# A decode block with its two small inputs in one layout, loaded by two transfers, and its output stored by two queues

## Chip, core and metric

The kernel runs on one core of a Trainium2 chip. Five engines work side by side: TensorE (PE, its weight loads PEld), VectorE (DVE), ScalarE (ACT), GpSimd (POOL) and SyncE (SP), which here only issues transfers. Sixteen DMA engines move data between the chip's memory (HBM) and the on-chip buffer. The metric is the device time of one execution in microseconds (us); of several runs the median counts.

## What is computed

A transformer block for two sequences with one new token each (B = 2, D = 512): a modulated attention over a window of the key and value caches, then a modulated feed-forward layer. All data are float32.

```python
mod = (silu(c) @ w_mod).reshape(2, 6, 1, 512)
sa, ca, ga, sb, cb, gb = (mod[:, i] for i in range(6))
h = layernorm(x) * (1 + ca) + sa
q = heads(h @ wq)                      # 32 heads of 128, 8 key/value heads
k, v = k_cache[:, :, -4096:], v_cache[:, :, -4096:]
x = x + ga * (softmax(q k^T / sqrt(128)) v @ wo)
h = layernorm(x) * (1 + cb) + sb
x = x + gb * (silu(h @ w1) @ w2)       # w1: 512 x 1792, w2: 1792 x 512
```

The inputs that matter for the time are w_mod (6 MB), wq and wo (8 MB each), the two cache windows (32 MB each) and w1 and w2 (3.5 MB each). x and c are 2 x 512 numbers, 4 KB each, and so is the output.

## The kernel before

Every large load goes through a ring of eight buffers of 2 MB (`RING`, `stream`), and all are issued in order by SP: w_mod in four parts, wq in four, then for each of the eight key/value heads the keys and values of both sequences, then wo in four parts, w1 in three and w2 in five. A load is issued once the buffer eight places back in the ring has been used up.

A vector of 512 numbers is spread over the 128 partitions so that VectorE can turn it with its 32 x 32 transposes. There are two such layouts here. In both, one row out of sixteen partitions holds data (`rows8` picks these eight rows), four rows for each sequence. In the "channel" layout (`c_ch`, `x_ch`, lines 99 to 110) a row a holds, for each k from 0 to 3, the 32 channels that start at 128 k + 32 a; after a transpose, block k holds the channels of rows 128 k to 128 k + 127 of a weight matrix. So `load_rows` (line 72) loads the weight's rows in blocks of 128: partition p of block k holds row 128 k + p. In the "spread" layout (`x_sp`) row g holds the 128 consecutive channels from 128 g on; `turned` (line 268) transposes it reading every fourth column, so that block k holds the channels 4 p + k. The weights that go with it are loaded by `load_runs` (line 91): partition p holds consecutive rows of the matrix. wo, w1 and w2 are loaded like that; w_mod and wq are loaded by `load_rows`.

The head: SP issues the first quarter of w_mod (line 74), then c and x in the channel layout, one transfer for each sequence (line 107, four transfers with pieces of 32 numbers), then the rest of w_mod and wq. DVE transposes c (line 235), silu follows (ACT and DVE), and PE multiplies with w_mod: `m_ch` (line 246) gets shift and scale of the first normalization in the channel layout, which takes a strided view `ab` of the weights, and `m_sp` (line 249) the other four vectors in the spread layout. Meanwhile `moments` computes mean and variance of x. Lines 257 to 263 make the normalized, modulated h_a and its transpose hq_T, from which PE makes q (line 285).

The middle: for each head, DVE transposes the keys (line 337), PE makes the scores (349), ACT the exponentials, and PE the weighted values (423). The order of these instructions is written out by hand (`keep_in_program_order`).

The end: the attention output goes through wo (550, 561). x is loaded a second time, now in the spread layout (line 474, issued between wo and w1), and turned into xT for the second normalization. PE multiplies with w1 (595) and w2 (631, 643); DVE multiplies the result with the gate and adds x (`yo`, lines 653 and 654). SP stores yo with one transfer (line 656).

Of the kernel before, what the change touches and what calls it, by code (L numbers as in the profile page):

```python
# [10 lines left out]
ALU = mybir.AluOpType  # L11
AX = mybir.AxisListType

P = 128
B, D = 2, 512
HQ, HKV, DH = 32, 8, 128
# [7 lines left out]
def adaln_block(  # L24
# [16 lines left out]

    nc = tc.nc
    SK = k_cache.shape[2]
    W = min(4096, max(256, SK // 4))
# [14 lines left out]
    def const(shape, name):  # L63
        return consts.tile(shape, F32, name=name)

    def bank(tag, name):
        return (psum1 if tag in "CO" else psum).tile([P, 512], F32, tag=tag, name=name)

    def stream(name):
        return ring.tile([P, 4096], F32, tag="st", name=name)  # L70

    def load_rows(name, w, k, width):
        t = stream(f"{name}{k}")[:, :width]
        nc.sync.dma_start(t, w[k * P : (k + 1) * P, :])
        return t

    def load_k(b, h):
        t = stream(f"k{h}_{b}")
        nc.sync.dma_start(
            t, k_cache[b, h, SK - W :, :].rearrange("(p n) d -> p (n d)", p=P)  # L80
        )
        return t
# [8 lines left out]
    def load_runs(name, w, per, lo, hi):  # L91

        e = w.shape[1]
        t = stream(f"{name}{lo}")[:, : (hi - lo) * e].rearrange("p (q e) -> p q e", e=e)
        nc.sync.dma_start(t, w.rearrange("(p q) e -> p q e", q=per)[:, lo:hi, :])
        return t


    x2 = x.rearrange("b s d -> (b s) d")
    x_sp, x_ch, c_ch = const([P, P], "x_sp"), const([P, P], "x_ch"), const([P, P], "c_ch")  # L100
    for t in (c_ch, x_ch, x_sp):
        nc.vector.memset(t, 0.0)
    wm = [load_rows("wm", w_mod, 0, 6 * D)]
    rows8 = lambda t: t.rearrange("(ab r) m -> ab r m", r=16)[:, 0, :]
    for t, src in ((c_ch, c), (x_ch, x2)):
        for b in range(B):
            nc.sync.dma_start(
                rows8(t)[b : 2 * 4 : 2, :].rearrange("a (k c) -> a k c", k=4),
                src[b, :].rearrange("(k a c) -> a k c", k=4, a=4),
            )  # L110
    wm += [load_rows("wm", w_mod, k, 6 * D) for k in range(1, 4)]
    wqt = [load_rows("wq", wq, k, HQ * DH) for k in range(4)]


    ident = const([P, P], "ident")
# [47 lines left out]
    for m in range(4):  # L163
        nc.gpsimd.affine_select(
            out=quad,
# [27 lines left out]

    oTn = const([P, 32, 32], "oTn")
    nc.gpsimd.memset(oTn, 0.0)
    mod_ch = const([P, 2, P], "mod_ch")
    mod_sp = const([P, 4, P], "mod_sp")
    x1 = const([P, P], "x1")

    def silu_exp(t, name, shape):  # L200

        e = once.tile(shape, F32, tag="silu", name=name)
        nc.vector.tensor_scalar(e, t, -1.0, 87.0, op0=ALU.mult, op1=ALU.min)
        nc.scalar.activation(e, e, AF.Exp)
        nc.vector.tensor_scalar(e, e, 1.0, None, op0=ALU.add)
        nc.vector.reciprocal(e, e)
        return e

    def moments(t, name):

        st = work.tile([P, 6], F32, tag="st6", name=f"st_{name}")
        nc.vector.bn_stats(st, t)
        mv = work.tile([P, 2], F32, tag="mv", name=f"mv_{name}")
        nc.vector.bn_aggr(mv, st)  # L214
        avgm = avg.rearrange("p a r -> p (a r)")
        sm = bank("B", f"mean_{name}")
        nc.tensor.matmul(sm[:, 0:1], avgm, mv[:, 0:1], start=True, stop=True)  # L217
        mean = work.tile([P, 1], F32, tag="mean", name=f"m_{name}")
        nc.vector.tensor_copy(mean, sm[:, 0:1])
        dm = work.tile([P, 2], F32, tag="dm", name=f"dm_{name}")  # L220
# [12 lines left out]

    cT = const([P, 4, 32], "cT")
    nc.vector.transpose(cT.rearrange("p k r -> p (k r)"), c_ch)
    sg = silu_exp(cT, "sgc", [P, 4, 32])
    scT = const([P, 4, 32], "scT")
    nc.vector.tensor_mul(scT, cT, sg)
    m_ch = bank("A", "m_ch")[:, : 2 * P]
    m_sp = bank("D", "m_sp")  # L240
    for k in range(4):
        ab = wm[k][:, : 2 * D].rearrange("p (s k a c) -> p a s k c", s=2, k=4, a=4)
        cd = wm[k][:, 2 * D :].rearrange("p (s g m) -> p g s m", s=4, g=4)
        for g in range(4):
            r = slice(32 * g, 32 * g + 32)
            nc.tensor.matmul(m_ch[r, :], scT[:, k, :], ab[:, g], start=(k == 0), stop=(k == 3))
        for g in range(4):
            r = slice(32 * g, 32 * g + 32)
            nc.tensor.matmul(m_sp[r, :], scT[:, k, :], cd[:, g], start=(k == 0), stop=(k == 3))  # L249
        if k == 0:  # L250
            mean_a, rstd_a = moments(x_ch, "a")
            xn = once.tile([P, P], F32, tag="xp", name="xn_a")
            nc.vector.tensor_scalar(
                xn, x_ch, mean_a, rstd_a, op0=ALU.subtract, op1=ALU.mult
            )

    nc.vector.tensor_copy(mod_ch[:, 0, :], m_ch[:, :P])
    nc.vector.tensor_scalar(mod_ch[:, 1, :], m_ch[:, P:], 1.0, None, op0=ALU.add)
    h_a = once.tile([P, P], F32, tag="pr", name="h_a")
    nc.vector.tensor_mul(h_a, xn, mod_ch[:, 1, :])  # L260
    nc.vector.tensor_add(h_a, h_a, mod_ch[:, 0, :])
    hq_T = const([P, 4, 32], "hq_T")
    nc.vector.transpose(hq_T.rearrange("p k r -> p (k r)"), h_a)
    nc.scalar.copy(mod_sp.rearrange("p s m -> p (s m)"), m_sp)
    nc.gpsimd.tensor_scalar(mod_sp[:, 2, :], mod_sp[:, 2, :], 1.0, None, op0=ALU.add)
    ga, sb, cb1, gb = (mod_sp[:, s, :] for s in range(4))

    def turned(t, name):
        o = const([P, 4, 32], name)
        nc.vector.transpose(o, t.rearrange("p (m k) -> p k m", k=4))  # L270
        return o


    hT, uT = const([P, 4, 32], "hT_b"), const([P, F // P, 32], "uT")
# [6 lines left out]
    for k in range(4):  # L281
        wv = wqt[k].rearrange("p (n s g m) -> p n g s m", n=2, s=4, g=G)
        for n in range(2):
            for g in range(G):
# [4 lines left out]
                    start=(k == 0),  # L289
                    stop=(k == 3),  # L290
                )
    for n in range(2):
        qT = once.tile([P, D], F32, tag="wide", name=f"qT{n}").rearrange("p (s j r) -> p s j r", s=4, r=32)
        nc.vector.transpose(qT.rearrange("p s j r -> p (s j r)"), q_ps[n])  # L294
        for g in range(G):
            r = slice(32 * g, 32 * g + 32)
# [8 lines left out]
        for i in range(4):  # L305
            r = slice(32 * i, 32 * i + 32)
# [160 lines left out]
    collect(HKV - 1)  # L467

    gaT, sbT, cbT = turned(ga, "gaT"), turned(sb, "sbT"), turned(cb1, "cbT")
    nc.vector.tensor_copy(hT[:, :, 1:32:16], sbT[:, :, 0:32:16])  # L470
    ax = once.tile([P, P], F32, tag="ax", name="ax")
    for q0 in range(0, 32, 8):
        wot.append(load_runs("wo", wo, 32, q0, q0 + 8))
    nc.sync.dma_start(rows8(x_sp), x2.rearrange("b (g m) -> g b m", m=P))
    xT = turned(x_sp, "xT")
    w1t = []
    for lo, hi in ((0, 2), (2, 3), (3, 4)):
# [17 lines left out]
    for r in (0, 64):  # L495
# [4 lines left out]
            start=True,  # L500
            stop=True,
# [46 lines left out]
    for q in range(24):  # L548
        g = q % 4
# [4 lines left out]
            start=(q < 4),  # L554
            stop=(q >= 20),
# [3 lines left out]
    for q in range(24, 32):  # L559
        for g in range(4):  # L560
# [4 lines left out]
                start=(q == 24),  # L565
                stop=(q == 31),
# [26 lines left out]
    for k in range(4):  # L593
        for g in range(4):
# [4 lines left out]
                start=(k == 0),  # L599
                stop=(k == 3),  # L600
# [16 lines left out]
    for b in range(B):  # L617
# [5 lines left out]
            op0=ALU.mult,  # L623
            op1=ALU.add,
# [4 lines left out]
    for tt in range(WIDE):  # L629
        g = tt % 4  # L630
# [4 lines left out]
            start=(tt < 4),  # L635
            stop=(tt >= WIDE - 4),
# [4 lines left out]
    for tt in range(WIDE, T2):  # L641
        for g in range(4):
# [4 lines left out]
                start=(tt == WIDE),  # L647
                stop=(tt == T2 - 1),
# [3 lines left out]
    yo = once.tile([P, P], F32, tag="yo", name="yo")  # L652
    nc.vector.tensor_mul(yo, y, gb)
    nc.vector.tensor_add(yo, yo, x1)
    of = out.rearrange("b s d -> (b s) d")
    nc.sync.dma_start(of.rearrange("b (g m) -> g b m", m=P), rows8(yo))


_INS = ["A_x", "A_k_cache", "A_v_cache", "A_wq", "A_wo", "B_w1", "B_w2", "c", "w_mod"]
# [24 lines left out]
```

## Time and profile before

| What | Value |
|---|---|
| Median of 3 runs | 237.28 us (236.99 to 237.31) |
| The profiled execution's own time | 236.89 us |
| Its span in the profile | 235.0 us |
| Read from HBM | 97.53 MB, 415 GB/s over the span |
| Mean granted clock of TensorE | 0.869 |
| DMA queue of SP | 7592 packets, 97.54 MB |

The span runs from the first to the last event of the profile; the time of a run has some 1.9 us more. "DMA share" in the views is the mean busy share of the sixteen DMA engines in a stretch; since packets overlap it can pass 1. A line such as "A <- B: 1.0" says that A sat idle for 1.0 us until B released it. SPq marks instructions in SP's queue, where the length of a DMA line is the time that issuing takes, not that of the transfer.

### The profile page before, as it was taken

Reading aid. Unit: us, or ns where it says so; the run is one execution under the profiler, and the core shown is the slowest. Engines: PE = TensorE matmul, PEld = TensorE weight load, DVE = VectorE, ACT = ScalarE, POOL = GpSimd, SP = SyncE. Lnnn points to the kernel's source line nnn. Section 1 sums busy time; section 2 is a strip of 40 time slices with the busy share of each in tenths; the row PEclk is TensorE's granted clock in tenths of the full one; section 3 lists DMA queues with packets and bytes.
Section 4 is the critical chain, followed back from the end, with each engine's and each line's share of the span. In section 5 each row is a group of like instructions: output and inputs, shape, how many; then the busy total and the mean of one; then the engine's idle time right before and its main releaser. Section 6 shows DMA issues by size and latency. Waiting matters only on the chain.

```text
span 235.0 us, 2644 instructions
## 1 busy us (share of the span) xinstructions
PE 146.5 (62%) x1094; PEld 45.9 (20%) x1094; DVE 114.6 (49%) x176; ACT 25.4 (11%) x56; POOL 10.3 (4%) x30
## 2 busy tenths in 40 slices
PE   0086546367187577667549519626743967788993
PEld 0032101101011121121112102111211222335332
DVE  0634000793694792693892792595298050002130
ACT  2200000100300200200200200200020021003210
POOL 8600000100000000000000000000000000000000
PEclk9999975759869997999976967965985799999999
DMA  6999999999999999999999999999999999999991
GB/s 253 426 438 427 427 438 427 424 439 427 429 441 424 427 438 427 429 438 424 429 435 429 427 432 432 432 429 432 428 429 429 429 432 429 432 426 422 421 412 56
DMA packets 7603, 97.69 MB, mean 416 GB/s; under 512 B 920, under 2 KB 936, under 8 KB 1576
## 3 DMA queue, kind: packets, MB, share of 16 engines
q1 hardware_dynamic: 7592, 97.54, 97.5%
q8 instruction: 8, 0.13, 0.2%
q14 instruction: 3, 0.02, 0.0%
HBM read 97.53 MB, written 0.00 MB: 415 GB/s over the span
## 4 chain that ended last, share of the span: by engine, by line
DMA 64%; DVE 22%; PE 10%; ACT 2%; issue 1%; SPq 1%; DVEq 0%
DVE kT L337 16%; DMA wo<-in_A_wo_dram 14%; DMA k<-in_A_k_cache_dram 14%; DMA v<-in_A_v_cache_dram 13%; DMA wq<-in_A_wq_dram 13%; DMA w<-in_B_w_dram 7%; PE s L349 5%; DMA wm<-in_w_mod_dram 3%; DVE zp L395 2%; PE o L423 2%; PE q L285 1%; DVE xp L393 1%; ACT pr L381 1%; DVE mx L359 1%; ACT L381 1%
## 5 line engine op out<-in xcount | busy, mean ns | idle before, releaser
L337 DVE STREAM_TRANSPOSE kT<-k 128x1024 f32<-128x1024 f32 x64 | 73.7, 1210 | 1.6 <-DMA k<-in_A_k_cache_dram 1.6
L349 PE MATMUL s<-kT,qbd 128*32 128x512 f32 x256 | 44.5, 670 | 11.2 <-DVE kT L337 11.1
L423 PE MATMUL o<-v,ptb 128*32 128x512 f32 x256 | 38.5, 730 | 19.8 <-DMA v<-in_A_v_cache_dram 19.3
L359 DVE TENSOR_REDUCE mx<-s 128x1 f32<-128x512 f32 x8 | 5.5, 691 | 40.1 <-PE s L349 40.1
L349 PEld LDWEIGHTS s<-kT,qbd 128*32 128x32 f32 x256 | 11.1, 126 | 45.8 <-issue 24.1
L285 PE MATMUL q<-wq,hq_T 128*32 128x512 f32 x64 | 11.2, 836 | 10.1 <-DMA wq<-in_A_wq_dram 10.1
L423 PEld LDWEIGHTS o<-v,ptb 128*32 128x32 f32 x256 | 8.1, 124 | 35.8 <-issue 33.1
L402 PE MATMUL pT<-zp,id 128*32 128x256 f32 x64 | 5.6, 418 | 13.9 <-DVE zp L395 13.9
L379 ACT COPY bias<-bp 128x1 f32<-128x1 f32 x8 | 1.3, 159 | 111.9 <-PE bp L377 111.9
L537 PE MATMUL junk<-selh,id 128*32 128x256 f32 x46 | 11.3, 380 | 0.0
L294 DVE STREAM_TRANSPOSE qT<-q 128x512 f32<-128x512 f32 x2 | 1.4, 718 | 18.6 <-PE q L285 18.3
L395 DVE TENSOR_TENSOR zp<-xp,group 128x1024 f32<-128x1024 f32 x8 | 9.8, 1225 | 0.2
L393 DVE STREAM_TRANSPOSE xp<-pr 128x512 f32<-128x512 f32 x8 | 5.6, 701 | 4.4 <-ACT pr L381 4.4
L217 PE MATMUL mean_a<-mv_a,avg 128*128 128x1 f32 x2 | 0.6, 362 | 10.6 <-DVE mv_a L214 10.6
L361 PE MATMUL mT<-ident,mx 128*1 128x128 f32 x16 | 3.0, 270 | 6.4 <-DVE mx L359 6.4
L550 PE MATMUL acc_o<-wo,oTn 128*32 128x512 f32 x48 | 5.8, 598 | 1.9 <-DMA wo<-in_A_wo_dram 1.6
L537 PEld LDWEIGHTS junk<-selh,id 128*32 128x32 f32 x46 | 5.0, 110 | 6.7 <-issue 3.5
L438 PE MATMUL o_all<-ob,selh 128*64 128x128 f32 x64 | 5.7, 304 | 0.8 <-ACT ob L432 0.8
L270 DVE STREAM_TRANSPOSE xT<-x_sp 128x128 f32<-128x128 f32 x1 | 0.4, 403 | 11.8 <-DMA x_sp<-in_A_x_dram 11.8
L432 ACT COPY ob<-o 128x512 f32<-128x512 f32 x8 | 4.7, 585 | 10.3 <-PE o L423 10.3
L285 PEld LDWEIGHTS q<-wq,hq_T 128*32 128x32 f32 x64 | 2.1, 128 | 18.8 <-DMA wq<-in_A_wq_dram 12.5
L249 PE MATMUL m_sp<-wm,scT 128*32 128x512 f32 x32 | 5.7, 796 | 0.0
(132 smaller groups left out, 95.0 us busy)
## 6 DMA issues: line engine op xcount, KB each, us to landing
k<-in_A_k_cache_dram SPq DMA_DIRECT2D x16, 2048.0 KB, 30.2
v<-in_A_v_cache_dram SPq DMA_DIRECT2D x16, 2048.0 KB, 31.5
wq<-in_A_wq_dram SPq DMA_DIRECT2D x4, 2048.0 KB
wo<-in_A_wo_dram SPq DMA_DIRECT2D x4, 2048.0 KB, 32.3
wm<-in_w_mod_dram SPq DMA_DIRECT2D x4, 1536.0 KB, 10.2
w<-in_B_w_dram SPq DMA_DIRECT2D x2, 1024.0 KB, 23.2
w<-in_B_w_dram SPq DMA_DIRECT2D x1, 1792.0 KB
w<-in_B_w_dram SPq DMA_DIRECT2D x2, 896.0 KB
```

The source lines that it names most:

```text
L249: nc.tensor.matmul(m_sp[r, :], scT[:, k, :], cd[:, g], start=(k == 0), stop=(k == 3))
L285: nc.tensor.matmul(q_ps[n][32 * g : 32 * g + 32, :], hq_T[:, k, :], wv[:, n, g], start=(k == 0), stop=(k == 3),)
L337: inorder(nc.vector.transpose(kT[h, b][:, :, 8 * n4 : 8 * n4 + 8, :].rearrange("p j n k -> p n j k"), kt[h, b][:, n4 * 1024 : (n4 + 1) * 1 ...
L349: inorder(nc.tensor.matmul(s_ps[h][r : r + 32, :], qbd[h // 4][:, h % 4, b, j, :], kT[h, b][:, j, 16 * c : 16 * c + 16, :], start=(j == 0) ...
L359: inorder(nc.vector.tensor_reduce(mx, s_ps[h], axis=AX.X, op=ALU.max))
L393: inorder(nc.vector.transpose(xp, pr[h]))
L395: inorder(nc.vector.tensor_mul(zp, xp[:, None, :, 0:16].to_broadcast([P, 4, 16, 16]), group[:, :, None, None].to_broadcast([P, 4, 16, 16]),))
L402: inorder(nc.tensor.matmul(tp[32 * i : 32 * i + 32, :], id4, zp.rearrange("p a s x -> p (a s) x")[:, :, 4 * i : 4 * i + 4], start=True, st ...
L423: inorder(nc.tensor.matmul(o_ps[h][32 * c : 32 * c + 32, :], ptb[h % 2][:, 256 * b + 32 * w : 256 * b + 32 * w + 32], vt[h, b][:, 512 * w ...
L438: inorder(nc.tensor.matmul(o_all[r : r + 64, :], selh[:, m, HQ - G - G * h : 3 * HQ - G - G * h], o_sb[h][:, m * DH : (m + 1) * DH], start ...
L537: inorder(nc.tensor.matmul(junk[0:32, :256], id4, selh.rearrange("p m y -> p (m y)")[:, :256], start=True, stop=True,))
L550: inorder(nc.tensor.matmul(acc[32 * g : 32 * g + 32, :], oTn[:, q, :], wot[q // 8][:, q % 8, :], start=(q < 4), stop=(q >= 20),))
```

## The change

The channel layout is given up. c and x are each loaded once, in the spread layout (`c_sp`, `x_sp`), by one transfer for both sequences, with pieces of 128 numbers. The second load of x, between wo and w1, is gone. w_mod and wq are loaded by `load_runs` in single rows: partition p of part k holds row 4 p + k, where it held row 128 k + p. `turned` serves c and h_a too, and the first normalization's shift and scale come out in the spread layout (`m_a`, `mod_a`). The number and shape of the matrix products stay. The output is stored by two transfers, the rows of the first sequence from SP's queue and those of the second from ACT's.

```diff
-    x_sp, x_ch, c_ch = const([P, P], "x_sp"), const([P, P], "x_ch"), const([P, P], "c_ch")
-    for t in (c_ch, x_ch, x_sp):
+    x_sp, c_sp = const([P, P], "x_sp"), const([P, P], "c_sp")
+    for t in (c_sp, x_sp):
         nc.vector.memset(t, 0.0)
-    wm = [load_rows("wm", w_mod, 0, 6 * D)]
+    row4 = lambda name, w, k: load_runs(name, w, 4, k, k + 1)[:, 0, :]
+    wm = [row4("wm", w_mod, 0)]
     rows8 = lambda t: t.rearrange("(ab r) m -> ab r m", r=16)[:, 0, :]
-    for t, src in ((c_ch, c), (x_ch, x2)):
-        for b in range(B):
-            nc.sync.dma_start(
-                rows8(t)[b : 2 * 4 : 2, :].rearrange("a (k c) -> a k c", k=4),
-                src[b, :].rearrange("(k a c) -> a k c", k=4, a=4),
-            )
-    wm += [load_rows("wm", w_mod, k, 6 * D) for k in range(1, 4)]
-    wqt = [load_rows("wq", wq, k, HQ * DH) for k in range(4)]
+    for t, src in ((c_sp, c), (x_sp, x2)):
+        nc.sync.dma_start(rows8(t), src.rearrange("b (g m) -> g b m", m=P))
+    wm += [row4("wm", w_mod, k) for k in range(1, 4)]
+    wqt = [row4("wq", wq, k) for k in range(4)]
...
-    cT = const([P, 4, 32], "cT")
-    nc.vector.transpose(cT.rearrange("p k r -> p (k r)"), c_ch)
+    cT = turned(c_sp, "cT")
...
-        ab = wm[k][:, : 2 * D].rearrange("p (s k a c) -> p a s k c", s=2, k=4, a=4)
+        ab = wm[k][:, : 2 * D].rearrange("p (s g m) -> p g s m", s=2, g=4)
...
-            mean_a, rstd_a = moments(x_ch, "a")
+            mean_a, rstd_a = moments(x_sp, "a")
...
-    nc.vector.transpose(hq_T.rearrange("p k r -> p (k r)"), h_a)
+    hq_T = turned(h_a, "hq_T")
...
-    nc.sync.dma_start(rows8(x_sp), x2.rearrange("b (g m) -> g b m", m=P))
     xT = turned(x_sp, "xT")
...
-    of = out.rearrange("b s d -> (b s) d")
-    nc.sync.dma_start(of.rearrange("b (g m) -> g b m", m=P), rows8(yo))
+    for b, queue in enumerate((nc.sync, nc.scalar)):
+        queue.dma_start(out[b, 0, :].rearrange("(g m) -> g m", m=P), rows8(yo)[b : 2 * 4 : 2, :])
```

More of the change, by code (lines that the diff above doesn't have):

```diff
@@ L70, in stream @@
         return ring.tile([P, 4096], F32, tag="st", name=name)
[L72 to L75, printed above, removed]
     def load_k(b, h):
@@ L195, in adaln_block @@
     nc.gpsimd.memset(oTn, 0.0)
-    mod_ch = const([P, 2, P], "mod_ch")
+    mod_a = const([P, 2, P], "mod_a")
     mod_sp = const([P, 4, P], "mod_sp")
@@ L231, in moments, with turned @@
         return mean, rstd
-    cT = const([P, 4, 32], "cT")
-    nc.vector.transpose(cT.rearrange("p k r -> p (k r)"), c_ch)
+    def turned(t, name):
+        o = const([P, 4, 32], name)
+        nc.vector.transpose(o, t.rearrange("p (m k) -> p k m", k=4))
+        return o
+    cT = turned(c_sp, "cT")
     sg = silu_exp(cT, "sgc", [P, 4, 32])
@@ L238, in adaln_block @@
     nc.vector.tensor_mul(scT, cT, sg)
-    m_ch = bank("A", "m_ch")[:, : 2 * P]
+    m_a = bank("A", "m_a")[:, : 2 * P]
     m_sp = bank("D", "m_sp")
     for k in range(4):
-        ab = wm[k][:, : 2 * D].rearrange("p (s k a c) -> p a s k c", s=2, k=4, a=4)
+        ab = wm[k][:, : 2 * D].rearrange("p (s g m) -> p g s m", s=2, g=4)
         cd = wm[k][:, 2 * D :].rearrange("p (s g m) -> p g s m", s=4, g=4)
@@ L245, in adaln_block @@
             r = slice(32 * g, 32 * g + 32)
-            nc.tensor.matmul(m_ch[r, :], scT[:, k, :], ab[:, g], start=(k == 0), stop=(k == 3))
+            nc.tensor.matmul(m_a[r, :], scT[:, k, :], ab[:, g], start=(k == 0), stop=(k == 3))
         for g in range(4):
@@ L250, in adaln_block @@
         if k == 0:
-            mean_a, rstd_a = moments(x_ch, "a")
+            mean_a, rstd_a = moments(x_sp, "a")
             xn = once.tile([P, P], F32, tag="xp", name="xn_a")
             nc.vector.tensor_scalar(
-                xn, x_ch, mean_a, rstd_a, op0=ALU.subtract, op1=ALU.mult
+                xn, x_sp, mean_a, rstd_a, op0=ALU.subtract, op1=ALU.mult
             )
-    nc.vector.tensor_copy(mod_ch[:, 0, :], m_ch[:, :P])
-    nc.vector.tensor_scalar(mod_ch[:, 1, :], m_ch[:, P:], 1.0, None, op0=ALU.add)
+    nc.vector.tensor_copy(mod_a[:, 0, :], m_a[:, :P])
+    nc.vector.tensor_scalar(mod_a[:, 1, :], m_a[:, P:], 1.0, None, op0=ALU.add)
     h_a = once.tile([P, P], F32, tag="pr", name="h_a")
[L260 to L263, printed above, removed]
+    nc.vector.tensor_mul(h_a, xn, mod_a[:, 1, :])
+    nc.vector.tensor_add(h_a, h_a, mod_a[:, 0, :])
+    hq_T = turned(h_a, "hq_T")
     nc.scalar.copy(mod_sp.rearrange("p s m -> p (s m)"), m_sp)
```

4 lines of the change are left out of this document (removed).

## The prediction

> **What bounds the kernel now.** The page comes first: its busy shares, the slices of the DMA rows, and the chain of waits.
>
> ```profile
> span 235.0 us, 2644 instructions
> PE 146.5 (62%) x1094; PEld 45.9 (20%) x1094; DVE 114.6 (49%) x176; ACT 25.4 (11%) x56; POOL 10.3 (4%) x30
> DMA  6999999999999999999999999999999999999991
> DMA packets 7603, 97.69 MB, mean 416 GB/s; under 512 B 920, under 2 KB 936, under 8 KB 1576
> DMA 64%; DVE 22%; PE 10%; ACT 2%; issue 1%; SPq 1%; DVEq 0%
> ```
>
> The reader sees that no compute engine is busy for more than 62% of the span, while the DMA row is full from the second slice to the last but one. The chain still gives DVE 22% and PE 10%: whenever a load waits for a buffer, the chain runs through the engine that frees it. That would matter only if the transfers ever ran dry, so the next view is the DMA share and rate stretch by stretch (columns: stretch, its length, five engines, granted clock, DMA share, GB/s).
>
> ```profile
> 1.60:2.00 0.40, 0.00 (x0) 0.00 (x0) 0.00 (x0) 0.40 (x1) 0.40 (x2) 1.00 1.94 338
> 3.00:6.50 3.50, 0.00 (x0) 0.00 (x0) 0.00 (x0) 0.00 (x0) 3.50 (x10) 1.00 1.04 431
> 6.50:8.00 1.50, 0.00 (x0) 0.00 (x0) 0.91 (x5) 0.00 (x0) 1.50 (x3) 1.00 0.96 401
> 8.00:18.00 10.00, 5.88 (x36) 2.58 (x40) 4.81 (x18) 1.85 (x3) 1.44 (x3) 1.00 1.01 430
> 18.00:37.00 19.00, 10.88 (x84) 2.32 (x76) 2.45 (x9) 0.58 (x1) 0.53 (x1) 0.86 1.01 430
> 40.00:180.00 140.00, 84.97 (x570) 23.39 (x564) 95.76 (x109) 14.99 (x39) 0.94 (x4) 0.83 1.01 431
> 195.00:213.00 18.00, 14.51 (x112) 5.50 (x104) 0.88 (x3) 2.12 (x3) 0.00 (x0) 1.00 1.01 433
> 213.00:229.00 16.00, 14.05 (x151) 6.38 (x150) 4.15 (x19) 2.49 (x5) 0.00 (x0) 1.00 0.99 416
> 229.00:230.00 1.00, 0.98 (x26) 0.67 (x28) 0.00 (x0) 0.21 (x1) 0.00 (x0) 1.00 0.67 270
> 230.00:231.20 1.20, 1.11 (x37) 0.59 (x30) 0.00 (x0) 0.00 (x0) 0.00 (x0) 1.00 0.24 90
> 231.20:233.50 2.30, 0.39 (x8) 0.12 (x8) 0.58 (x2) 0.00 (x0) 0.00 (x0) 1.00 0.00 0
> 233.50:234.00 0.50, 0.00 (x0) 0.00 (x0) 0.00 (x0) 0.00 (x0) 0.00 (x0) 1.00 0.04 8
> 234.00:235.00 1.00, 0.00 (x0) 0.00 (x0) 0.00 (x0) 0.00 (x0) 0.00 (x0) 1.00 0.00 0
> ```
>
> From 3 us to 229 us the sixteen DMA engines are at a share of 0.96 to 1.04 and move 401 to 433 GB/s, whichever load is on the wire. So the time is a sum of three pieces: a start of some 2 to 3 us, the bytes at about 430 GB/s, and a tail after the last load. An edit counts only if it changes the bytes, their rate, the start or the tail.
>
> **The change, part by part.** The first part is the head of SP's queue. Columns here are start, length, engine, line and operation.
>
> ```profile
> 0.73 0.40 SPq L74 DMA_DIRECT2D wm<-in_w_mod_dram  x1
> 1.19 1.29 SPq L107 DMA_DIRECT2D c_ch<-in_c_dram  x2
> 2.53 1.09 SPq L107 DMA_DIRECT2D x_ch<-in_A_x_dram  x2
> 3.65 1.40 SPq L74 DMA_DIRECT2D wm<-in_w_mod_dram  x3
> 181.60 0.58 SPq L474 DMA_DIRECT2D x_sp<-in_A_x_dram  x1
> ```
>
> Four small issues (1.29 + 1.09 = 2.38 us) become two in the form of the row at L474 (2 x 0.58 = 1.16 us), so the second w_mod load is issued about 1.2 us sooner, near 2.4 us. The first load is issued at the same 0.73 us, and it alone keeps the engines at 431 GB/s until 6.5 us; the second is in the queue by then either way. Gain of the earlier issue: nothing, covered by the first w_mod load; without that cover it would be the 1.2 us. The transfers themselves are another matter: the stretch of 6.5 to 8 us, in which the small pieces pass, runs at 401 instead of 430 GB/s, a loss of 1.5 x (1 - 401/430) = 0.10 us. Two loads in place of four should keep half of it: -0.05 us, bounds 0 and -0.10.
>
> The second part is the way in which w_mod and wq are read. A partition still reads one piece of 12 or 16 KB, but neighbours in the tile are now 48 or 64 KB apart in memory instead of adjacent. These loads are 4 x 1536 KB + 4 x 2048 KB = 14.7 MB, 34 us at 431 GB/s. The nearest row is the wo load, which reads 16 KB pieces 64 KB apart (eight rows of 2 KB out of 32 for each partition): its stretch, 195 to 213 us, shows 433 GB/s against 431 for the adjacent k and v pieces of 40 to 180 us and 430 for wq now. Value taken: 0. Bounds: at 433 GB/s the 14.7 MB would gain 0.16 us; at the slowest loading stretch of the trace, 416 GB/s (213 to 229 us, the narrower pieces of w1 and w2), they would lose 1.2 us.
>
> The Trainium skill has a rule against this edit ("DMA: Bandwidth & Descriptors", section "Latency and other measured facts"): a pitch between rows that is a large power of two slows copies, 207 GB/s at 512 KiB where a padded pitch gave 214. Applied at its full 3.4% to 34 us that would be an estimate of +1.15 us; the rows of wo at a 64 KB pitch do not agree, and no run here has a pitch as large as that page's.
>
> The third part is the work between the small loads and q. Transposes that read with a stride cost a little more:
>
> ```profile
> 7.09 0.31 DVE L235 STREAM_TRANSPOSE cT<-c_ch 128x128 f32<-128x128 f32 x1 [5.75 <-DMA c_ch<-in_c_dram]
> 21.37 0.31 DVE L263 STREAM_TRANSPOSE hq_T<-h_a 128x128 f32<-128x128 f32 x1
> 213.28 0.40 DVE L270 STREAM_TRANSPOSE xT<-x_sp 128x128 f32<-128x128 f32 x1 [11.79 <-DMA x_sp<-in_A_x_dram]
> 16.14 5.23 SPq L79 DMA_DIRECT2D k<-in_A_k_cache_dram  x4
> L285 PE MATMUL q<-wq,hq_T 128*32 128x512 f32 x64 | 11.2, 836 | 10.1 <-DMA wq<-in_A_wq_dram 10.1
> ```
>
> cT and hq_T take the form of xT: 0.40 instead of 0.31 us, +0.09 each. In the order of the changed kernel xT itself (0.40 us) moves up between the constants and the first statistics, and the bias of silu stands ahead of the constants. So the DVE head shifts by +0.6 us at most, and by less where silu's exponential now overlaps the constants. Two things wait behind it. PE's q products wait 10.1 us for wq, longer than any such shift. SP's first k loads (16.14 us) wait for the modulation products to free w_mod's buffers; the DMA engines then still hold wq, which keeps them at 430 GB/s to 37 us, a cover of 20 us. Cost: 0; without wq in flight it would be up to 0.6 us. The matmuls into m_a read adjacent columns instead of strided ones, in equal number and shape, under the same cover.
>
> The fourth part is the x load taken out between wo and w1 (0.58 us of SP's queue). It and xT end nothing: SP has the w loads waiting on buffers, and these land late after their issue for want of bandwidth, not of issue.
>
> ```profile
> w<-in_B_w_dram SPq DMA_DIRECT2D x1, 768.0 KB, 20.1
> w<-in_B_w_dram SPq DMA_DIRECT2D x1, 512.0 KB, 16.5
> DVE aoT L572 <- PE ao L561: 2.5, 1, 2.5
> ```
>
> With 16.5 to 20 us from issue to landing, a w load that is issued half a microsecond sooner only queues longer. DVE's next wait after xT was for PE's output product, which stays. Cost and gain 0.
>
> The fifth part is the tail, the one place where nothing covers.
>
> ```profile
> 230.53 1.06 PE L643 MATMUL acc_y<-w,uT 128*32 128x128 f32 x24
> 231.66 0.29 DVE L653 TENSOR_TENSOR yo<-acc_y,mod_sp 128x128 f32<-128x128 f32 x1 [5.73 <-PE acc_y L643]
> 231.98 0.29 DVE L654 TENSOR_TENSOR yo<-yo,x 128x128 f32<-128x128 f32 x1
> 232.30 0.59 SPq L656 DMA_DIRECT2D out_dram<-yo  x1
> SPq L680 <- DMA out_dram<-yo: 1.0, 1, 1.0
> 228.62 0.58 ACT L522 COPY acc_y_sb<-acc_yw 128x512 f32<-128x512 f32 x1 [3.51 <-PE acc_yw L631]
> 181.22 0.33 SPq L95 DMA_DIRECT2D wo<-in_A_wo_dram  x1
> ```
>
> From the end of yo (232.27 us) the store costs 0.59 us of issue, then 1.0 us in which SP waits for its landing; some 1.1 us more pass to the end of the span. After the change each queue issues half the store with one dimension fewer. SP's half lies between 0.33 us (the plain two-dimensional issue of wo) and 0.59 us: a gain of 0 to 0.26 us. ACT's half is an operation the trace does not show; ACT itself is free, its last copy ending at 229.20 us. From below, it costs what SP's does. From above, it comes 0.59 us behind SP's, if the two issues are served one after the other. The end waits for the later one, so the tail moves by -0.26 to +0.59 us. The four kinds of small issues in the trace all took 0.52 to 0.65 us on average, so I hold each half near 0.55 us, side by side: -0.05 us.
>
> The sum, against the profiled execution's 236.89 us (span 235.0 and 1.9 around it): 236.89 - 0.05 (head) + 0 (pitch) - 0.05 (tail) = 236.8 us. That execution ran 0.39 us below the median of the runs shown, so against the median the same sum is 237.28 - 0.1 = 237.2 us.
>
> **The rivals.** *The small loads hold up the engines that end last (faster).* The tail is ragged: between 229 and 231.2 us the engines do 0.67 x 1.0 + 0.24 x 1.2 = 0.96 us of work in 2.2 us, so the last of them ends 1.2 us after an even finish. If the 0.10 us lost on sixteen engines is really 1.6 us on four of them, that is 0.4 us each, and if those are the last, three fifths of five loads saved gives 0.25 us; with SP's 0.26 us in the tail that is 237.28 - 0.5 = 236.8 us. For it: 920 packets under 512 B. Against it: nothing here says which engines end last, and both halves are needed to get past 0.2%.
>
> *ACT's half of the store lands last (slower).* Place: the end of the kernel, after yo. Price: up to 0.59 us, one issue, if the halves are served in turn or if ACT's first transfer takes that much longer than SP's last. It decides as soon as ACT's half lands later than SP's gains. 237.28 - 0.05 + 0.59 = 237.8 us. For it: no transfer leaves ACT's queue anywhere in the trace. Against: ACT is idle, and the halves touch different rows.
>
> *The spread rows cost bandwidth (slower).* 1.2 us by the 416 GB/s stretch: 238.4 us. Against it stands the wo stretch, of the very same pattern as wq's.
>
> *The change does nothing that can be told.* This is the forecast's own class, and the reason for it is the DMA row.
>
> **How the numbers follow.** No change to be told (within 0.2%, or 0.47 us, which is about what a measurement of this kernel can tell from none): 0.51, at 237.2 us. The fast engines' rival: 0.22, at 236.8 us and below. ACT's store: 0.19, at 237.8 us. The spread rows and anything else on the DMA engines: 0.08, near 238.4 us. So faster 0.22, same 0.51, slower 0.27. The range adds the gains' bounds (0.10 + 0.16 + 0.26 = 0.52) below, with a little more for the rival, and reaches above past the store's bound and part of the way to the spread rows: 236.6 to 238.2 us. The forecast's own range is 236.9 to 237.6 us.
>
> **What would show each step.** Head: the three further w_mod issues near 2.4 us, the stretch of 6.5 to 8 us above 401 GB/s, and k still issued near 16 us. Pitch: 430 GB/s in the stretches 8 to 18 and 18 to 37 us; 420 or less would prove the third rival. Tail: yo ending within 0.2 us of 232.27; if it ends 0.3 us sooner at equal rates, the first rival holds. Store: one issue on SP and one on ACT after yo, with 2.6 to 2.75 us from the end of yo to the end of the span; 3.2 us or more there is the ACT rival. The forecast as a whole is wrong if the time leaves 236.8 to 237.75 us, above all if the DMA row shows a slice under 9 before the last.

## The result, and the profile after

The changed kernel takes 237.90 us (median of 7 runs, 237.80 to 238.02) against 237.21 us for the kernel before on the same chip (7 runs, 236.99 to 237.31). The ratio is 1.0031, with a 95% interval of 1.0022 to 1.0040: some 0.7 us slower. That is inside the outer range of 236.6 to 238.2 us, but it is not the forecast of no change, and it lies outside 236.8 to 237.75 us, beyond which the prediction called itself wrong. The profiled execution took 237.90 us with a span of 235.8 us. The profiled execution of before (236.89 us) ran 0.3 us under its median, so that differences between these two profiles come out a little too large. One of the 27 runs of the kernel before that stand beside e5 to e8 below took 289 us and is in no ratio.

The page of the changed kernel first: the DMA rows, the queues, and the chain of waits.

```profile
span 235.8 us, 2641 instructions
DMA  7999999999999999999999999999999999999991
DMA packets 7539, 97.69 MB, mean 414 GB/s; under 512 B 848, under 2 KB 872, under 8 KB 1512
q10 hardware_dynamic: 8, 0.00, 0.0%
DMA 64%; DVE 23%; PE 8%; ACT 2%; issue 1%; POOL 0%; SPq 0%; POOLq 0%
```

The picture is the same: a DMA row that is full from end to end. Fewer small packets pass (848 under 512 B instead of 920), and q10 is new: ACT's queue. So the loss is in the rate, the start or the tail. The stretches of before, now for the changed kernel (stretch, length, five engines, granted clock, DMA share, GB/s):

```profile
3.00:6.50 3.50, 0.00 (x0) 0.00 (x0) 0.00 (x0) 0.00 (x0) 3.50 (x10) 1.00 0.98 402
6.50:8.00 1.50, 0.00 (x0) 0.00 (x0) 0.91 (x4) 0.00 (x0) 1.50 (x3) 1.00 0.99 377
8.00:18.00 10.00, 6.28 (x44) 2.79 (x48) 4.79 (x21) 1.85 (x3) 1.44 (x3) 1.00 1.01 424
18.00:37.00 19.00, 10.04 (x76) 2.25 (x68) 2.45 (x9) 0.58 (x1) 0.53 (x1) 0.84 1.01 433
40.00:180.00 140.00, 84.38 (x564) 23.40 (x556) 95.31 (x108) 14.98 (x39) 0.94 (x4) 0.82 1.01 431
213.00:229.00 16.00, 14.02 (x151) 6.28 (x150) 3.73 (x18) 2.66 (x4) 0.00 (x0) 1.00 1.00 421
```

Until 18 us, while w_mod is on the wire, the rate is 402, 377 and 424 GB/s where it was 431, 401 and 430 (the first two of these vary much from execution to execution, as the experiments show). From 18 us on, where wq, the caches and the last weights pass, nothing is lost. The head of SP's queue and the tail (start, length, engine, line, operation; the last line is a wait):

```profile
2.53 1.43 SPq L88 DMA_DIRECT2D wm<-in_w_mod_dram  x3
4.01 4.02 SPq L88 DMA_DIRECT2D wq<-in_A_wq_dram  x4
15.74 5.04 SPq L72 DMA_DIRECT2D k<-in_A_k_cache_dram  x4
...
232.53 0.29 DVE L641 TENSOR_TENSOR yo<-yo,x 128x128 f32<-128x128 f32 x1
232.85 0.58 SPq L644 DMA_DIRECT2D out_dram<-yo  x1
232.86 1.42 ACTq L644 DMA_DIRECT2D out_dram<-yo  x1
SPq L668 <- DMA out_dram<-yo: 1.2, 1, 1.2
```

The w_mod loads are issued at 2.53 instead of 3.65 us, and k at 15.74 instead of 16.14 us: no issue is late. Yet yo ends at 232.82 instead of 232.27 us, 0.55 us later, and from there to the end of the span it is 3.0 instead of 2.7 us. The issue on ACT takes 1.42 us against 0.58 us on SP. So there are two places to look at: w_mod's loads and the store.

### The profile page after: what moved, and what is told of

It reads as the page before. It is cut to its first block, busy times and chain, and to the rows that moved or that the text cites. A ratio compares the mean times of both kernels' runs of the same rounds, so it can differ in the third digit from the quotient of the medians.

```text
span 235.8 us, 2641 instructions
## 1 busy us (share of the span) xinstructions
PE 147.0 (62%) x1094; PEld 46.0 (20%) x1094; DVE 114.1 (48%) x175; ACT 25.4 (11%) x56; POOL 10.3 (4%) x30
## 4 chain that ended last, share of the span: by engine, by line
DMA 64%; DVE 23%; PE 8%; ACT 2%; issue 1%; POOL 0%; SPq 0%; POOLq 0%
DMA k<-in_A_k_cache_dram 26%; DVE kT L325 16%; DMA wo<-in_A_wo_dram 14%; DMA wq<-in_A_wq_dram 13%; DMA w<-in_B_w_dram 8%; PE s L337 5%; DMA wm<-in_w_mod_dram 3%; DVE zp L383 3%; DVE xp L381 1%; ACT pr L369 1%; DVE mx L347 1%; PE acc_o L537 1%; DVE qT L282 1%; ACT L369 1%; PE mT L349 1%
## 5 line engine op out<-in xcount | busy, mean ns | idle before, releaser
L411 PE MATMUL o<-v,ptb 128*32 128x512 f32 x256 | 40.5, 765 | 21.9 <-DMA v<-in_A_v_cache_dram 21.4
L337 PE MATMUL s<-kT,qbd 128*32 128x512 f32 x256 | 42.2, 659 | 9.5 <-DVE kT L325 9.5
L273 PE MATMUL q<-wq,hq_T 128*32 128x512 f32 x64 | 10.6, 789 | 10.3 <-DMA wq<-in_A_wq_dram 10.3
L537 PE MATMUL acc_o<-wo,oTn 128*32 128x512 f32 x48 | 7.3, 753 | 1.1 <-DMA wo<-in_A_wo_dram 0.7
L365 PE MATMUL bp<-negscale,mrow 1*128 1x1 f32 x16 | 3.0, 256 | 4.2 <-DVE mrow L358 4.2
```

The costliest lines, as they stand in the source:

```text
L273: nc.tensor.matmul(q_ps[n][32 * g : 32 * g + 32, :], hq_T[:, k, :], wv[:, n, g], start=(k == 0), stop=(k == 3),)
L337: inorder(nc.tensor.matmul(s_ps[h][r : r + 32, :], qbd[h // 4][:, h % 4, b, j, :], kT[h, b][:, j, 16 * c : 16 * c + 16, :], start=(j == 0) ...
L411: inorder(nc.tensor.matmul(o_ps[h][32 * c : 32 * c + 32, :], ptb[h % 2][:, 256 * b + 32 * w : 256 * b + 32 * w + 32], vt[h, b][:, 512 * w ...
L537: inorder(nc.tensor.matmul(acc[32 * g : 32 * g + 32, :], oTn[:, q, :], wot[q // 8][:, q % 8, :], start=(q < 4), stop=(q >= 20),))
```

## The experiments

Each kernel was timed against the kernel before on the same chip, 11 runs of it (5 for e7, one for e11) against some 27 to 33. The interval is about 0.2 us to either side (0.3 for e7). The ratio comes from all these runs and is not quite the quotient of the two medians; a price in us below is the ratio's excess times 237 us. e3 to e6, e9 to e11, e14 and e15 leave out the pairing of weight rows and channels, so their output is another; apart from the edit, their loads and products are those of the kernel that they start from, in number and size. The diffs are shortened; in every kernel c and x are issued right behind the first load.

| Run | Edit | Median us (before) | Ratio | 95% interval |
|---|---|---|---|---|
| e1 | changed kernel, one store | 237.56 (237.07) | 1.0017 | 1.0009 to 1.0026 |
| e2 | before, stores on SP and ACT | 237.38 (237.07) | 1.0012 | 1.0004 to 1.0021 |
| e3 | changed kernel, adjacent rows | 237.51 (237.07) | 1.0018 | 1.0009 to 1.0027 |
| e4 | before, w_mod spread | 237.42 (237.07) | 1.0011 | 1.0002 to 1.0020 |
| e5 | before, wq spread | 237.24 (237.24) | 1.0003 | 0.9994 to 1.0012 |
| e6 | before, two small loads | 236.98 (237.24) | 0.9992 | 0.9983 to 1.0001 |
| e7 | before, two stores on SP | 237.82 (237.24) | 1.0032 | 1.0019 to 1.0044 |
| e8 | before, one store on ACT | 237.24 (237.24) | 1.0003 | 0.9995 to 1.0012 |
| e9 | changed kernel, adjacent rows, one store | 237.24 (237.18) | 1.0003 | 0.9994 to 1.0012 |
| e10 | before, wq's rows in w_mod's place | 237.06 (237.18) | 0.9996 | 0.9987 to 1.0004 |
| e11 | before, wq ahead, w_mod spread | 237.19 (237.18) | one run | none |
| e12 | mixed kernel | 237.19 (237.18) | 1.0001 | 0.9992 to 1.0010 |
| e13 | changed kernel, wq ahead, one store | 236.95 (237.21) | 0.9989 | 0.9981 to 0.9998 |
| e14 | before, one part of wq ahead, w_mod spread | 237.04 (237.21) | 0.9993 | 0.9984 to 1.0002 |
| e15 | before, w_mod parts 1 to 3 spread | 237.47 (237.21) | 1.0011 | 1.0002 to 1.0020 |

### The store (e1, e2, e7, e8)

e1 takes the second store out of the changed kernel, e2 puts it into the kernel before, e7 issues both halves from SP, e8 issues the whole store from ACT.

```diff
 e1: changed kernel
-    for b, queue in enumerate((nc.sync, nc.scalar)):
-        queue.dma_start(out[b, 0, :].rearrange("(g m) -> g m", m=P), rows8(yo)[b : 2 * 4 : 2, :])
+    of = out.rearrange("b s d -> (b s) d")
+    nc.sync.dma_start(of.rearrange("b (g m) -> g b m", m=P), rows8(yo))
 e2, e7: kernel before
-    of = out.rearrange("b s d -> (b s) d")
-    nc.sync.dma_start(of.rearrange("b (g m) -> g b m", m=P), rows8(yo))
+    for b, queue in enumerate((nc.sync, nc.scalar)):      # e7: (nc.sync, nc.sync)
+        queue.dma_start(out[b, 0, :].rearrange("(g m) -> g m", m=P), rows8(yo)[b : 2 * 4 : 2, :])
 e8: kernel before
-    nc.sync.dma_start(of.rearrange("b (g m) -> g b m", m=P), rows8(yo))
+    nc.scalar.dma_start(of.rearrange("b (g m) -> g b m", m=P), rows8(yo))
```

> The changed kernel with the output stored by one transfer from SP, as before the change. Theory H (head and tail both pay: the two first w_mod loads of the changed kernel land 0.4 to 0.6 us late, and ACT's store, whose issue takes 1.42 us against SP's 0.58, ends the kernel 0.2 us later): 0.2 us less than the changed kernel, about 237.7 us, +0.5 us on the kernel before (ratio 1.002), and 2.75 us from the end of yo to the end of the span. Rival T (the tail pays for all of it): the time of the kernel before, 237.2 us. Rival N (the second store costs nothing, since SP waits for both anyhow): 237.9 us.

> The kernel before with the output stored by two transfers, from SP and ACT; nothing else is changed. Theory H: +0.2 us (237.4 us, ratio 1.001), an issue on ACT of about 1.4 us, 2.95 us from the end of yo to the end of the span, and the head as before. Rival T: +0.7 us (237.9 us). Rival N: 237.2 us.

> The kernel before with the output stored by two transfers, both from SP, one after the other. Theory A (ACT is the slow one: its issue takes 1.41 us): the second issue costs one SP issue, 0.58 us, less what the halves save, so +0.4 to +0.6 us (ratio 1.002). Rival (any second store costs the same 0.3 us through the second wait at the end): +0.3 us, ratio 1.0012.

> The kernel before with the one store issued by ACT instead of SP. Theory A: ACT's issue takes 1.4 us against 0.59 and the end comes 0.3 to 0.8 us later, ratio 1.0012 to 1.0035. Rival (the cost is in having two stores, not in ACT): 237.1 us, ratio 1.000.

e1 keeps a loss of 0.4 us (1.0017), so the tail is not all of it. e2 has 1.0012, or 0.28 us: the second store has its price without any other edit. e7 pays more, 0.76 us (1.0032, five runs; 0.45 to 1.04), of which one more issue on SP is some 0.57 us (1.15 us for two). e8 was to be 0.3 to 0.8 us slower if ACT were the slow one, and is not (1.0003). The tails of the three kernels, e2 first: when the issues ran, and two stretches with the bytes of the store in them.

```profile
232.31 0.58 SPq L657 DMA_DIRECT2D out_dram<-yo  x1
232.31 1.41 ACTq L657 DMA_DIRECT2D out_dram<-yo  x1
...
233.40:233.80 0.40, 0.00 (x0) 0.00 (x0) 0.00 (x0) 0.00 (x0) 0.00 (x0) 1.00 0.02 5
233.80:234.20 0.40, 0.00 (x0) 0.00 (x0) 0.00 (x0) 0.00 (x0) 0.00 (x0) 1.00 0.03 5
```

e7, both halves from SP:

```profile
232.29 1.15 SPq L657 DMA_DIRECT2D out_dram<-yo  x2
...
233.50:234.00 0.50, 0.00 (x0) 0.00 (x0) 0.00 (x0) 0.00 (x0) 0.00 (x0) 0.50 0.02 4
234.00:234.50 0.50, 0.00 (x0) 0.00 (x0) 0.00 (x0) 0.00 (x0) 0.00 (x0) 0.50 0.02 4
```

e8, the whole store from ACT:

```profile
232.27 1.14 ACTq L656 DMA_DIRECT2D out_dram<-yo  x1
...
233.40:233.80 0.40, 0.00 (x0) 0.00 (x0) 0.00 (x0) 0.00 (x0) 0.00 (x0) 1.00 0.04 10
233.80:234.20 0.40, 0.00 (x0) 0.00 (x0) 0.00 (x0) 0.00 (x0) 0.00 (x0) 1.00 0.00 0
```

ACT's issue is long, 1.14 us, but alone it puts all 4 KB on the wire before 233.80 us. With SP's half issued at the same instant, ACT's issue grows to 1.41 us, and one half crosses in the next stretch, in a window of its own. The packets of the trace say which: in e2 the eight packets of SP's queue (q1) run from 233.52 to 233.61 us, the eight of ACT's (q10) from 233.89 to 233.97 us. The halves do not land side by side; ACT's follows SP's. In e8 and in e2 alike ACT's first packet starts some 0.16 us after its issue ends (233.56 after 233.41 us, 233.89 after 233.72 us), so the delay is in the longer issue; why the issue grows is not shown. Against the last packet of the kernel before (233.64 us) the store ends 0.33 us later in e2, and 0.54 us later in e7 (234.18 us).

### The rows (e3, e4, e5, e9)

```diff
 e3: changed kernel (e9: with e1's edit too)
-    row4 = lambda name, w, k: load_runs(name, w, 4, k, k + 1)[:, 0, :]
+    row4 = lambda name, w, k: load_rows(name, w, k, w.shape[1])
 e4: kernel before
-    wm = [load_rows("wm", w_mod, 0, 6 * D)]
+    wm = [row4("wm", w_mod, 0)]            # and so for k = 1 to 3
 e5: kernel before
-    wqt = [load_rows("wq", wq, k, HQ * DH) for k in range(4)]
+    wqt = [row4("wq", wq, k) for k in range(4)]
```

> The changed kernel with w_mod and wq read in adjacent rows, as before the change (partition p of part k holds row 128 k + p); the products then pair the wrong rows with the channels, so the output is another, with the same instructions. Theory P (the spread rows slow the first loads): the stretch of 3 to 8 us is back at the 431 and 401 GB/s of before, and the time falls by about 0.5 us to 237.4 us (ratio 1.001). Rival S (the small loads of 512 B pieces or the earlier issues of w_mod and wq slow them): the stretch of 3 to 6.5 us stays near 402 GB/s and the time at 237.9 us.

> The kernel before with w_mod alone read in spread rows (partition p of part k holds row 4 p + k), wq as before; the modulation then pairs the wrong rows with the channels, so the output is another, with the same instructions. Theory P: +0.5 us (237.7 us, ratio 1.002), 402 GB/s from 3 to 6.5 us and below 390 from 6.5 to 8. Rival S: 237.2 us, 431 GB/s from 3 to 6.5 us.

> The kernel before with wq alone read in spread rows, w_mod as before; q then pairs the wrong rows with the channels, so the output is another. Theory F (spread rows cost only at the start of the program, in w_mod): 237.1 us, ratio 1.000, 427 to 433 GB/s from 18 to 37 us, as in the changed kernel. Rival (spread rows cost wherever they stand): +0.3 us or more, ratio 1.0013, and below 425 GB/s in that stretch.

> The changed kernel with both suspected costs undone: w_mod and wq in adjacent rows, and one store from SP; the products pair the wrong rows, so the output is another. Theory P+D (spread w_mod rows and the second store are the whole loss): ratio 0.999 to 1.0003, 236.9 to 237.2 us on a chip where the kernel before takes 237.1. Rival R (something else in the new head costs some 0.2 to 0.3 us, as the run with adjacent rows and two stores leaves room for): 1.0008 or more.

w_mod in spread rows costs 0.26 us by itself (e4, 1.0011), half of what was expected; wq in spread rows costs nothing that can be told (e5). With the rows adjacent again and the two stores kept, e3 still has 1.0018, more than the 1.0012 of the stores alone; the intervals overlap, but it left room for a third cost. With both undone, e9 has 1.0003, so no third cost is seen; its interval reaches 1.0012, so one of 0.2 us is made unlikely and not excluded. In the traces the first 8 us scatter from execution to execution: from 3 to 6.5 us the nine kernels that start with w_mod in adjacent rows have 392 to 431 GB/s (e3 had 399, which by its expectation spoke for the rival). So the stretches from 3 and 8 to 22 us are read. The kernel before:

```profile
3.00:22.00 19.00, 8.85 (x68) 3.42 (x68) 7.42 (x28) 2.44 (x4) 6.71 (x15) 1.00 1.01 429
8.00:22.00 14.00, 8.85 (x68) 3.42 (x68) 6.51 (x25) 2.44 (x4) 1.71 (x4) 1.00 1.01 432
```

The changed kernel:

```profile
3.00:22.00 19.00, 8.66 (x68) 3.39 (x68) 8.00 (x30) 2.44 (x4) 6.97 (x15) 1.00 1.00 418
8.00:22.00 14.00, 8.66 (x68) 3.39 (x68) 7.09 (x29) 2.44 (x4) 1.97 (x4) 1.00 1.01 426
```

e4, the kernel before with w_mod spread:

```profile
3.00:22.00 19.00, 8.16 (x68) 3.28 (x68) 7.78 (x30) 2.44 (x4) 6.97 (x15) 1.00 1.00 417
8.00:22.00 14.00, 8.16 (x68) 3.28 (x68) 7.21 (x28) 2.44 (x4) 1.97 (x4) 1.00 1.01 425
```

e9, the changed kernel with both undone:

```profile
3.00:22.00 19.00, 9.17 (x68) 3.46 (x68) 7.63 (x29) 2.44 (x4) 6.79 (x15) 1.00 1.00 428
8.00:22.00 14.00, 9.17 (x68) 3.46 (x68) 6.58 (x28) 2.44 (x4) 1.79 (x4) 1.00 1.02 434
```

With w_mod spread the engines move 417 and 418 GB/s from 3 to 22 us, with adjacent rows 428 and 429, at nearly the same share of busy time. From 8 to 22 us the two groups stand apart in every kernel that starts with w_mod: 429 to 434 GB/s in the nine with adjacent rows, 424 to 427 in the four with spread ones (the changed kernel, e1, e4, e15). From 3 us on it is 423 to 431 against 416 to 421. 19 x (1 - 418/429) = 0.49 us for these two profiles, next to the 0.55 us by which yo came late.

The trace also has the length of every packet, and w_mod's are the only ones of 12 KB. So its four loads can be read by themselves: mean ns of the 128 packets of each, and what they take above 460 ns, summed over 32 packets, an even share for each of the sixteen engines.

| Kernel | w_mod stands | Mean ns, loads 1 to 4 | Above 460 ns, us |
|---|---|---|---|
| before | first, adjacent | 533, 472, 460, 460 | 0.68 |
| e9 | first, adjacent | 550, 460, 460, 460 | 0.72 |
| changed kernel | first, spread | 549, 494, 460, 470 | 1.07 |
| e4 | first, spread | 570, 482, 460, 469 | 1.14 |
| e15 | first, loads 2 to 4 spread | 555, 476, 465, 461 | 0.95 |
| e10 | first, 64 KB pitch | 542, 482, 463, 460 | 0.87 |
| e11, e14 | behind adjacent wq, spread | 460, 460, 460, 460 | 0.00 |
| e13 | behind spread wq, spread | 473, 461, 472, 460 | 0.22 |

The first load is slow in whichever pattern; what the spread rows add is mostly in the loads behind it. Over all kernels that start with w_mod it is 0.58 to 0.83 us with adjacent rows and 0.95 to 1.21 with spread ones: the engines are not starved, their packets take longer.

### The small loads (e6)

```diff
-        for b in range(B):
-            nc.sync.dma_start(
-                rows8(t)[b : 2 * 4 : 2, :].rearrange("a (k c) -> a k c", k=4),
-                src[b, :].rearrange("(k a c) -> a k c", k=4, a=4),
-            )
+        nc.sync.dma_start(rows8(t), src.rearrange("b (g m) -> g b m", m=P))
```

> The kernel before with c and x loaded at the head by two transfers with 512 B pieces instead of four with 128 B pieces, everything else as before; the channels then meet the wrong rows, so the output is another. Theory G (the small loads are a gain, as the prediction had it): -0.05 to -0.1 us, ratio 0.9996, which this measurement can't tell from 1, but more than 410 GB/s from 6.5 to 8 us. Rival (what is left of the changed kernel's loss in the run with adjacent rows, some 0.15 us, comes from the two loads or from issuing w_mod and wq sooner): +0.15 us, ratio 1.0006, and 400 GB/s or less from 3 to 6.5 us.

Ratio 0.9992, a gain of 0.2 us that just can't be told from none; the rival's loss (1.0006) is out. The rates decide nothing here: e6 has 434 GB/s from 6.5 to 8 us, the theory's sign, and 392 from 3 to 6.5 us, the rival's, and e5 with all four small loads has 434 and 396. Part of the gain is in the tail, which is shown below.

### Pitch or place (e10, e11, e13, e14, e15)

Why does w_mod suffer, and wq not? Its pitch is 48 KB and not 64 KB, and it stands first.

```diff
 e10: kernel before, w_mod's four loads
+    wide = wq[:, : 6 * D]
+    wm = [row4("wm", wide, k) for k in range(4)]
 e11: kernel before, all of wq ahead of w_mod
+    wqt = [load_rows("wq", wq, k, HQ * DH) for k in range(4)]
+    wm = [row4("wm", w_mod, k) for k in range(4)]
 e13: changed kernel with e1's edit, all of wq ahead of w_mod
+    wqt = [row4("wq", wq, k) for k in range(4)]
+    wm = [row4("wm", w_mod, k) for k in range(4)]
 e14: kernel before
+    wqt = [load_rows("wq", wq, 0, HQ * DH)]             # one part, the other three behind w_mod
+    wm = [row4("wm", w_mod, k) for k in range(4)]
 e15: kernel before
-    wm += [load_rows("wm", w_mod, k, 6 * D) for k in range(1, 4)]
+    wm += [row4("wm", w_mod, k) for k in range(1, 4)]
```

> The kernel before in which the four w_mod loads read the first 12 KB of wq's rows instead, row 4 p + k for partition p: the same position at the start and the same 12 KB pieces as the spread w_mod, at a pitch of 64 KB instead of 48 KB; the modulation is made from other numbers, so the output is another. Theory K (the pitch of 48 KB is what hurts, since wq and wo at 64 KB cost nothing): ratio 1.000, 429 to 432 GB/s from 6.5 to 37 us. Rival O (any spread rows hurt while they are the first loads of the program): ratio 1.0011, 424 to 427 GB/s in that stretch.

> The kernel before with wq loaded ahead of w_mod, and w_mod in spread rows; the modulation pairs the wrong rows, so the output is another, and the time is several us longer since the keys' buffers come free later, so only the rate is read. w_mod then passes between some 22 and 36 us. Theory K: that stretch is 1 to 3% below 430 GB/s, as w_mod's loads are at the start. Rival O: 430 GB/s.

> The changed kernel, computing the same result, with one store from SP and wq loaded ahead of w_mod. Theory L (spread rows are slow only in about the first 20 us; w_mod passed at full rate from 22 to 37 us when wq was ahead of it): the loss of w_mod is gone, but wq's spread rows now stand at the start; by the run that read wq's rows there (ratio 0.9996) they cost at most 0.1 us, so ratio 0.9995 to 1.0007. Rival K (the pitch of 48 KB costs wherever it stands): 1.0011 or more, as the changed kernel with one store had 1.0017.

> The kernel before with one adjacent part of wq as the first load, then w_mod in spread rows, then the rest of wq; the modulation pairs the wrong rows, so the output is another. Theory L (elapsed time counts): w_mod still passes mostly before 20 us, 417 to 424 GB/s from 3 to 22 us and 0.1 to 0.3 us lost, ratio 1.0005 to 1.0012. Rival V (only the very first load of the program must be adjacent): 426 to 429 GB/s from 8 to 22 us, ratio 1.0000.

> The kernel before with the first part of w_mod in adjacent rows and the other three in spread rows; the modulation pairs the wrong rows, so the output is another. Theory L: 0.1 to 0.25 us lost, ratio 1.0004 to 1.0010, 418 to 425 GB/s from 3 to 22 us. Rival V: ratio 1.0000, 428 GB/s from 8 to 22 us.

e10: the same pieces at 64 KB in the same place cost nothing (0.9996), which speaks for the pitch. e11 was expected to be several us longer and took 237.19 us, so even the keys' late issue stayed covered; its w_mod passed at full rate, which speaks for the place. e14 has one adjacent part of wq ahead, and w_mod then loses nothing (0.9993, 460 ns in all four loads) although it still passes mostly before 22 us: elapsed time is out. From 3 us on e14 has 419 GB/s, as the theory it refutes expected, but that is the first load: wq's first part takes 732 ns a packet, where 611 is usual for its 16 KB. That profile's last wq packet ends at 37.52 us, as in e15, which e14's time does not show. e15 has w_mod's own first part adjacent, and loses as much as e4 (1.0011): that only the very first load counts is out too. In e13, with all of wq ahead in spread rows, w_mod's packets are longer again, later in the program (0.22 us by the table). The stretch of 8 to 22 us in e10 and e15, and the one in which w_mod passes in e14, e11 and e13:

```profile
8.00:22.00 14.00, 7.92 (x68) 3.20 (x68) 7.28 (x27) 2.44 (x4) 1.98 (x4) 1.00 1.01 431
```

```profile
8.00:22.00 14.00, 8.90 (x68) 3.43 (x68) 6.47 (x24) 2.44 (x4) 1.66 (x4) 1.00 1.01 427
```

```profile
8.00:22.00 14.00, 8.25 (x52) 2.61 (x52) 3.26 (x12) 1.85 (x3) 1.54 (x4) 1.00 1.01 432
```

```profile
22.00:37.00 15.00, 8.36 (x48) 1.88 (x48) 0.00 (x0) 0.00 (x0) 0.00 (x0) 1.00 1.00 428
```

```profile
22.00:37.00 15.00, 5.78 (x48) 1.52 (x48) 0.00 (x0) 0.00 (x0) 0.00 (x0) 1.00 1.00 422
```

So neither the place alone nor the pitch alone decides. w_mod's spread rows were slow at the start (e4, the changed kernel), behind their own adjacent first part (e15) and, by the packets of one profile, behind spread parts of wq (e13, whose time shows no loss); they ran at full rate behind adjacent parts of wq (e11, e14). e10 is no clean zero either: its packets lie a little above those of the adjacent kernels, though its time shows no loss. That w_mod's spread rows at the head cost time is shown; why they do there and not behind adjacent rows of wq stays open.

### Two kernels with the same result (e12, e13)

e12 takes only the free parts: c in the channel layout by two transfers with w_mod in adjacent rows, x once in the spread layout with wq in spread rows, one store from SP.

```diff
 e12: changed kernel with e1's edit
-    wm = [row4("wm", w_mod, 0)]
+    wm = [load_rows("wm", w_mod, 0, 6 * D)]            # and so for k = 1 to 3
-    cT = turned(c_sp, "cT")
+    cT = const([P, 4, 32], "cT")
+    nc.vector.transpose(cT.rearrange("p k r -> p (k r)"), c_sp)   # c loaded as before the change
```

> A correct kernel made of the parts that cost nothing: c in the channel layout by two transfers, with w_mod in adjacent rows; x once, in the spread layout, with wq in spread rows; one store from SP. Theory P+D: no loss is left and two of five small loads are saved, 0.05 to 0.2 us less than the kernel before, ratio 0.9992 to 1.0, which may not be told from 1. Rival R: 1.0008 or more.

e12 equals the kernel before (1.0001, up to 1.0010), a second run that shows no third cost. e13, whose edit stands above, beats both kernels: 236.95 us, 0.9989 of the kernel before (0.9981 to 0.9998), some 0.26 us. Half of that is in its tail. Its store and the wait for it:

```profile
232.11 0.29 DVE L641 TENSOR_TENSOR yo<-yo,x 128x128 f32<-128x128 f32 x1
232.43 0.60 SPq L643 DMA_DIRECT2D out_dram<-yo  x1
SPq L667 <- DMA out_dram<-yo: 0.8, 1, 0.8
```

From the end of yo (232.40 us) to the end of the span (235.0 us) it takes 2.6 us instead of 2.7 us, and SP waits 0.8 instead of 1.0 us. e1, e6, e9 and e12, which also have fewer small transfers and one store from SP, show the same 0.8 us; e4, e5 and e10, which keep all five small loads, show 1.0 us. What makes the other half of e13's gain was not taken apart.

## Why the prediction went wrong

What bounds the kernel was right: the time is the start, the bytes at some 430 GB/s and the tail, and no compute engine moved it. Two terms of the sum were wrong. The prediction's own signs came out between its cases: 424 GB/s from 8 to 18 us, where 430 was expected and 420 would have proved the third rival; yo 0.55 us late, where 0.2 was allowed; 3.0 us from yo to the end, where 2.75 was the bound and 3.2 the sign of the ACT rival.

**Pitch.** The step that failed is "Value taken: 0", from the wo stretch at a 64 KB pitch. It held for wq, which has that very pattern (e5, 1.0003), but was carried over to w_mod, whose pitch is 48 KB and for which the trace had no row. w_mod measured +0.26 us (e4, interval 0.05 to 0.47), between the bounds of -0.16 and +1.2 us, and its packets took longer. The third rival was thus right in kind and five times too dear. The rule of the Trainium skill that was set aside ("DMA: Bandwidth & Descriptors", section "Latency and other measured facts", the slow pitches) speaks of large powers of two and has no figure below 512 KiB. The estimate of +1.15 us made from it for both weights does not hold here: 64 KB, a power of two, cost no time that can be told (e5, e10), and 48 KB, which is none, cost 0.26 us (e4). It pointed at the term that failed, but these runs do not bear out its reason.

**Tail.** The step that failed is "I hold each half near 0.55 us, side by side: -0.05 us". ACT's half lands behind SP's: +0.28 us (e2), inside the stated bounds of -0.26 and +0.59 us. The second rival named this mechanism, "if the halves are served in turn", at up to 0.59 us. Its other reason, that ACT's transfer is late for itself, is not borne out by e8 (1.0003).

**The head.** The earlier issue gave nothing, as predicted (issued at 2.53 us, covered). The term of -0.05 us for the small loads was worked out from one reading, 401 GB/s from 6.5 to 8 us, as if the small pieces made it. That reading was scatter: with the same four small loads this stretch has 442 (e2), 434 (e5), 476 (e7) and 435 GB/s (e8). e6 gained 0.2 us, right in sign, but not clear of none. The DVE shifts stayed covered: k was issued at 15.74 us, sooner than before. That the removal of the x load gives nothing agrees with e9, though there it is one edit among several.

**The sum.** 0.26 + 0.28 - 0.2 (e6) = 0.3 us by the single edits, each within 0.2 us, against 0.7 measured. The sum falls short. Taken the other way it closes: out of the changed kernel's 1.0031, undoing the store gives 1.0017 (e1, 0.33 us), undoing the rows 1.0018 (e3, 0.31 us), and undoing both 1.0003 (e9, 0.66 us). So the two costs add up and carry the loss. That they cost more there than alone is not shown to be more than the scatter; most of what is missing is e6's gain, of which e9, which saves the same small loads, shows nothing (1.0003). The first rival finds no support in e9 for the same reason; a smaller form of it is left open by e6.

The forecast put 0.27 on slower, split between the two mechanisms that both came true in part. What was not seen is that they add: 0.19 and 0.08 were counted as alternatives, though nothing in the kernel keeps them apart.

## What to carry to other kernels

In a kernel that is bound by transfers for its whole length, an edit of the loads is paid at the rate, not at the issue: look at what a load reads from memory before counting its instructions, and take a pattern as free only where a row shows that very pattern in that place. The small store at the end gained nothing from being split over two queues: its halves landed one behind the other. Rivals that can both be true belong together in the range.

## What was not expected

A store issued by ACT occupies it for 1.14 us (e8), twice SP's 0.59 us, and yet its last packet ends 1.45 us after yo, against 1.37 us from SP: the length of an issue is not the latency of its transfer. Loading wq ahead of w_mod delays the first key loads from 16 to 29 us and still costs nothing (e11, e13). The issue of these loads in e13:

```profile
29.37 10.15 SPq L72 DMA_DIRECT2D k<-in_A_k_cache_dram  x4
```
The first load of the program is slow whatever it reads: 524 to 570 ns a packet for w_mod against 460 later, 732 and 733 for wq in adjacent rows (e14, e11) and 683 in spread ones (e13) against 611; why is not shown. And the wait for the last store goes with transfers far ahead of it: 0.8 us with two or three small loads fewer, 1.0 us with all five; why is not shown.
